# A fixed order for the DMA queue, value sums in skewed quads, first weights on another queue, and scan banks apart, in a one-core scan-and-attention kernel

## The chip, the core and the metric

The kernel runs on one core of a Trainium2 chip. The metric is the device time of one execution in microseconds (us), as the median of several executions. The profile shows one execution; its span is about 1.5 to 1.7 us shorter than the time reported for the same execution.

The engines in the profile are: PE, the tensor engine's matmuls, and PEld, its weight loads; DVE, VectorE; ACT, ScalarE; POOL, GpSimd. SP is the Sync engine, which computes nothing here but issues nearly all DMAs. SPq and ACTq are the DMA issues on the Sync and the ScalarE queue. A DMA queue issues in order, as the traces here show it: an issue that has to wait for its data holds up all issues behind it (in e1 below, eight stores wait behind two copies until 119.3 us).

Executions of the kernel before differ by up to 3% among themselves (163.8 to 168.5 us over all chips used). Those over 1.5% above the fastest of their group are called slow and are left out of ratios; the slow ones show a mean granted tensor clock of 0.954 to 0.974 in the records, the fast ones mostly 0.976 to 0.988.

## The reference

Two independent parts read two inputs of 2048 positions by 448 features and write the two halves of one output.

```python
# part A: a diagonal complex state space, 448 states
Lam_bar = exp(dt * Lam)
Bu = x @ B_bar.T                       # complex
h_t = Lam_bar * h_{t-1} + Bu_t         # 2048 steps
a = 2 * real(h @ C.T) + x * Dskip
# part B: 16 heads of 28; each position sees 8 positions, 2 apart, backwards
q, k, v = split(x @ wqkv)
logits[s, w] = q[s] . k[s - 2*w] * scale      # w = 0..7, masked before the start
o[s] = sum_w softmax(logits)[s, w] * v[s - 2*w]
b = o @ wo
out = concatenate([a, b], axis=-1)
```

## The kernel before

The instructions of the tensor engine, VectorE and ScalarE are issued in the order in which the program calls them. The Sync queue is not in that list: a scheduler of the build chooses its order.

```python
with tc.manual_schedule(engines={ET.PE, ET.DVE, ET.Activation}):
    plan(a, b, cx, pool)
```

The loads at the start: three small parameter vectors and the skip vector on the ScalarE queue, all else on the Sync queue. `load_w(1)` and `load_w(0)` bring the key and query weights, each as a main DMA of 336 KB and a tail of 56 KB.

```python
    a.load_params()        # prow x3, drow x2, on nc.scalar
    b.load_x(0)            # two transposing DMAs
    b.load_w(1)
    b.load_w(0)
    b.load_x(1)
    # ... x 2 and 3, B, value weights, 32 transposing loads of A's x
```

The value projection writes `vd`, 16 positions to a partition, plus a halo of 14 that is copied from the neighbour partition by DMA (`halo`). The second copy is called after the last value projection, and after it come 8 loads of C and 24 small loads of wo.

```python
            b.proj_v(j, "A")
            if j == 8:
                b.halo(b.vd, 8, HALO)
            if j == 0:
                b.halo(b.vd, 0, 8)
                a.load_c()
                b.load_wo()
                a.setup_c()
```

The value sums on VectorE: for a block of positions, 8 products of attention weight and value, each added to the sum right after it is made. The first block has 8 positions (3584 elements a partition, called 8-wide below), then follow blocks of 4, 2 and 2. When a block is done, `turn` sends it through a transposing DMA into `oT` for the output projection.

```python
        acc = self.pvb[:, j0:j1]
        for w in range(W):
            off = HALO + j0 - DIL * w
            t_ = self.pvt[w % 2][:, 0:n] if w else acc
            V.tensor_tensor(t_, self.at[:, w, j0:j1, :].unsqueeze(2).to_broadcast([NCH, n, DH, H]),
                            self.vd[:, off:off + n], op=ALU.mult)
            yield
            if w:
                V.tensor_tensor(acc, acc, t_, op=ALU.add)
                ...   # turn at w == W - 1
                yield
    pv = chain(b.pv(0, 8), b.pv(8, 12), b.pv(12, 14), b.pv(14, 16))
```

The second half of the plan puts steps of `pv` between those of part A: local products (`u_ps`), the scan (`last`, `rot`, `scan`, `back`), corrections (`co`), outputs of A (`y`) and of B (`out`). The outputs of A leave through two buffers `ya`, those of B through two buffers `yb`.

```python
    run(pv, 6)
    loc((2, 4), (2, 5))
    r = a.regs("g3")              # PSUM banks of the scan, from the pool "mm" of the local products
    a.last(r[0])                  # -> rt on VectorE
    loc((1, 4), (1, 5), (0, 6), (2, 6))
    r_ = a.regs("rot")
    a.rot(r_[0], 0)
    # ... scan, back, groups, correct, with run(pv, 1) or run(pv, 2) between
    run(pv, 5)
    for a_ in range(4):
        a.y(a_, 3)
    a.correct(2, "A", range(7))
    for a_ in range(4):
        a.y(a_, 1)
    run(pv, 30)
    b.out(0)
    b.out(2)
    # ... y(.,0), out(4), out(6), out(8), out(10), y(.,2), out(12)
    run(pv, 99)
    b.out(14, "AV")
```

## Time and profile before

| | before |
|---|---|
| time, median of the first 3 runs | 165.15 us (165.13 to 167.45) |
| span of the profiled execution | 163.7 us |
| PE busy / DVE busy | 144.1 / 133.1 us |
| longest DVE wait after 10 us | 8.3 us, for the halo copy |
| longest PE wait after 10 us | 6.3 us, for scan inputs of DVE |
| DVE ends its value sums | 155.9 us |

First the busy times by stretch of the kernel before. Each row is a stretch in us from the span's start, its length, then the busy us of PE, PEld, DVE, ACT and POOL with the number of instructions, the granted clock, the DMA share and GB/s.

```profile
20.00:50.00 30.00, 29.84 (x219) 16.13 (x217) 27.06 (x34) 20.96 (x41) 0.00 (x0) 1.00 0.35 66
...
73.00:84.00 11.00, 11.00 (x53) 4.95 (x52) 2.74 (x3) 6.13 (x11) 0.00 (x0) 1.00 0.44 108
84.00:94.00 10.00, 4.47 (x33) 2.33 (x31) 9.93 (x7) 2.66 (x5) 0.00 (x0) 0.83 0.78 171
94.00:105.00 11.00, 9.26 (x56) 5.04 (x57) 9.96 (x13) 3.53 (x6) 0.00 (x0) 0.84 0.01 1
...
118.00:146.00 28.00, 27.62 (x179) 14.94 (x177) 27.52 (x32) 14.76 (x29) 0.00 (x0) 1.00 0.52 124
```

A different engine is full in each part. From 20 to 50 us it is PE (29.84 of 30). From 73 to 84 PE is full and DVE does 2.74 us of work in 11. From 84 to 94 it is the other way round, and in 94 to 105 the clock has fallen to a mean of 0.84. From then on DVE is nearly full. An average over the span (PE 88%, DVE 81%) hides that for 20 us one of the two always stood.

The waits tell why. The lines name who waited, for whom, the total in us, how often, and the longest.

```profile
DVE pvt L273 <- DMA vd<-vd: 8.3, 1, 8.3
...
PE u_ps L524 <- DVE rt L557: 6.3, 1, 6.3
...
PE gt L588 <- DVE gsc L572: 1.5, 1, 1.5
...
DVE gsc L572 <- PE rotA L565: 1.0, 1, 1.0
```

And the chain that ended last shows the cause (start, length, what), cut to a few pieces between 64 and 86 us:

```profile
65.50 0.61 SPq L342
...
67.53 0.64 SPq L123
...
78.25 0.60 SPq L186
...
78.90 4.46 DMA vd<-vd
...
83.46 2.04 DVE pvt L273
```

L342 are loads of C, L123 to L125 those of wo, L186 is the halo copy. The queue was issuing loads whose data PE first uses at 118.3 us (C) and 134.0 us (wo), while the copy that DVE needed at 75 us stood behind them. DVE then makes its products from 83.5 us on, and the scan inputs, which come after six of its steps, are late. On PE that looks like this (start, length, engine, line, operation, tiles, shapes; in brackets the idle time before and what ended it):

```profile
87.45 1.03 PE L524 MATMUL u_ps<-xaT,Bcat 128*128 128x512 bf16 x4
94.73 1.89 PE L524 MATMUL u_ps<-xaT,Bcat 128*128 128x512 bf16 x4 [6.26 <-DVE rt L557]
```

Four such matmuls take 1.03 us before the 6.3 us hole and 1.89 us after it. These are local products, which read nothing of the scan (their inputs are xaT and Bcat). By the kernel, their sums and the scan's share the four PSUM banks of "mm"; so what they waited for was most likely a bank that stayed full until DVE had read the scan's sum.

The start, in the chain of waits:

```profile
0.80 4.47 DMA xbT<-in_B_x_dram
...
5.28 3.99 DMA wqkv_nat<-in_B_wqkv_dram
...
9.32 5.40 PE qk_ps L168 x24
```

The DMAs of x and then of the weights hold the start; the projections are in full swing only at 9.3 us, when the last weights have landed.

### The profile page before, as it was taken

What the parts mean: (1) busy time and instruction counts of PE and PEld (TensorE: products, weight loads), DVE (VectorE), ACT (ScalarE), POOL (GpSimd) and SP (SyncE); (2) the same over time, 40 slices, a digit from 0 to 9 for tenths busy, and PEclk for the clock granted to TensorE, in tenths of its full rate; (3) what the DMA queues carried; (4) which work ended last, traced back from release to release, by engine and by line L of the source; (5) the groups of instructions that cost most, each with busy time, mean ns of one, the idle gap of its engine ahead of it and who ended that gap; (6) DMA issues with size and microseconds to landing.
All of it is one profiled execution on the core that took longest, in us unless ns stands there. A gap on an engine that the chain in (4) does not pass through costs nothing.

```text
span 163.7 us, 2533 instructions
## 1 busy us (share of the span) xinstructions
PE 144.1 (88%) x934; PEld 78.3 (48%) x934; DVE 133.1 (81%) x167; ACT 87.2 (53%) x162; POOL 10.8 (7%) x46
## 2 busy tenths in 40 slices
PE   6799799999999999999996089639899999999980
PEld 4346454555555665554452044515454555555540
DVE  0479998599999997493069979999999999999911
ACT  3158965686768577545554014208834745545360
POOL 8960000000000002000000000000000000000000
PEclk9999999999999999999999559999999999999998
DMA  5899982221222226632669400000009622946231
GB/s 100 215 201 193 228 136 58 45 63 35 62 57 40 45 55 107 112 77 52 175 165 207 95 0 0 4 0 0 0 30 162 149 84 84 224 144 175 80 114 56
DMA packets 42284, 15.67 MB, mean 96 GB/s; under 512 B 34771, under 2 KB 42017, under 8 KB 42271
## 3 DMA queue, kind: packets, MB, share of 16 engines
q1 hardware_dynamic: 42200, 15.50, 43.0%
q8 instruction: 7, 0.11, 0.3%
q14 instruction: 6, 0.05, 0.1%
q10 hardware_dynamic: 71, 0.01, 0.0%
HBM read 3.62 MB, written 3.67 MB: 45 GB/s over the span
## 4 chain that ended last, share of the span: by engine, by line
PE 51%; DVE 20%; DMA 10%; SPq 7%; issue 5%; ACT 4%; DVEq 0%; ACTq 0%
PE qk_ps L168 15%; PE y_ps L624 11%; PE wo_ps L305 8%; DVE pvt L273 6%; DVE pvb L277 4%; PE lg L214 4%; DVE pr L203 3%; PE co L599 3%; PE v_ps L182 3%; DMA xbT<-in_B_x_dram 3%; DMA vd<-vd 3%; DVE mat L482 2%; DMA wqkv_nat<-in_B_wqkv_dram 2%; SPq L125 2%; DMA out_dram<-ya 2%
## 5 line engine op out<-in xcount | busy, mean ns | idle before, releaser
L203 DVE TENSOR_TENSOR pr<-qT,kT 112x4096 bf16<-112x4096 bf16 (+1 forms) x20 | 36.2, 1859 | 3.5 <-PE lg L214 2.6
L273 DVE TENSOR_TENSOR pvt<-attn,vd 128x896 bf16<-128x896 bf16 (+2 forms) x28 | 30.4, 1084 | 8.3 <-DMA vd<-vd 8.3
L524 PE MATMUL u_ps<-xaT,Bcat 128*128 128x512 bf16 x112 | 28.4, 389 | 6.3 <-DVE rt L557 6.3
L168 PE MATMUL qk_ps<-xbT,wqkv_nat 128*112 128x512 bf16 x128 | 29.7, 382 | 2.3 <-DMA wqkv_nat<-in_B_wqkv_dram 1.3
L277 DVE TENSOR_TENSOR pvb<-pvb,pvt 128x896 bf16<-128x896 bf16 (+2 forms) x28 | 30.5, 1090 | 0.9
L624 PE MATMUL y_ps<-C,u 128*128 128x448 bf16 x112 | 23.8, 353 | 0.0
L168 PEld LDWEIGHTS <-wqkv_nat 128*112 128x112 bf16 x128 | 15.9, 130 | 15.1 <-issue 3.4
L532 ACT CAST u<-u_ps 128x512 bf16<-128x512 f32 x21 | 12.3, 586 | 16.5 <-PE u_ps L524 11.8
L524 PEld LDWEIGHTS <-Bcat 128*128 128x128 bf16 x112 | 10.7, 100 | 18.5 <-DVE rt L557 6.7
L627 ACT CAST ya<-y_ps 128x448 bf16<-128x448 f32 x16 | 8.5, 532 | 16.0 <-PE y_ps L624 14.0
L607 ACT CAST u<-co 128x512 bf16<-128x512 f32 x21 | 10.8, 618 | 7.1 <-PE co L603 7.1
L182 PE MATMUL v_ps<-wqkv_nat,xbT 128*128 128x448 bf16 x64 | 13.8, 358 | 0.0
L305 PE MATMUL wo_ps<-wo_p,oT 128*128 128x448 bf16 x64 | 13.1, 352 | 0.7 <-ACT oT L296 0.7
L624 PEld LDWEIGHTS <-u 128*128 128x128 bf16 x112 | 9.9, 98 | 7.3
L81 ACT CAST qT<-qk_ps 112x512 bf16<-112x512 f32 x16 | 9.3, 588 | 5.8 <-PE qk_ps L168 5.8
L81 ACT CAST vd<-v_ps 128x448 bf16<-128x448 f32 x16 | 8.5, 538 | 5.1 <-PE v_ps L182 5.1
L182 PEld LDWEIGHTS <-xbT 128*128 128x128 bf16 x64 | 8.8, 147 | 5.0 <-issue 2.5
L81 ACT CAST kT<-qk_ps 112x512 bf16<-112x512 f32 x16 | 9.2, 587 | 3.3 <-PE qk_ps L168 3.3
L81 ACT CAST yb<-wo_ps 128x448 bf16<-128x448 f32 x15 | 8.0, 532 | 4.1 <-PE wo_ps L305 3.6
L599 PE MATMUL co<-u,ident 128*128 128x512 bf16 x21 | 7.9, 378 | 2.1 <-DVE u L590 1.0
L214 PE MATMUL lg<-pr,onesW 112*32 112x512 bf16 x128 | 9.5, 383 | 0.2 <-DVE pr L203 0.2
L305 PEld LDWEIGHTS <-oT 128*128 128x128 bf16 x64 | 6.2, 97 | 6.7 <-ACT oT L296 0.9
(155 smaller groups left out, 153.3 us busy)
## 6 DMA issues: line engine op xcount, KB each, us to landing
out_dram<-ya SPq DMA_DIRECT2D x16, 112.0 KB, 1.7
out_dram<-yb SPq DMA_DIRECT2D x8, 224.0 KB, 2.3
wqkv_nat<-in_B_wqkv_dram SPq DMA_DIRECT2D x3, 336.0 KB, 3.7
vd<-vd SPq DMA_DIRECT2D x1, 784.0 KB
wo_p<-in_B_wo_dram SPq DMA_DIRECT2D x16, 42.0 KB, 1.9
vd<-vd SPq DMA_DIRECT2D x1, 588.0 KB, 4.9
xaT<-in_A_x_dram SPq DMA_TRANSPOSE x32, 2.4
bX<-in_A_B_re_dram SPq DMA_DIRECT2D x1, 392.0 KB, 5.6
```

The source lines that it names most:

```text
L81: nc.scalar.copy(out, in_)
L168: nc.tensor.matmul(ps[:], lhsT=self.wn[:, k, which, g * KP:(g + 1) * KP], rhs=self.xT[:, k, c * CH:(c + 1) * CH], start=(k == 0), stop=(k ...
L182: nc.tensor.matmul(ps[:], lhsT=xv[:, k, j, :], rhs=self.wn[:, k, 2, :], start=(k == 0), stop=(k == KT - 1))
L203: self.nc.vector.tensor_tensor(pr[:, :, g0:g1, :], self.qT[:, c, g0:g1].unsqueeze(1).to_broadcast([KP, 2, n, CH]), ks, op=ALU.mult)
L214: nc.tensor.matmul(lg[NW * g:NW * (g + 1), :], lhsT=self.onesW[:, NW - 4 - 4 * w:2 * NW - 4 - 4 * w], rhs=pr[:, i, g, :], start=(w == 0), ...
L273: V.tensor_tensor(t_, self.at[:, w, j0:j1, :].unsqueeze(2).to_broadcast([NCH, n, DH, H]), self.vd[:, off:off + n], op=ALU.mult)
L277: V.tensor_tensor(acc, acc, t_, op=ALU.add)
L305: nc.tensor.matmul(ps[:], lhsT=oT[:, NSL * (i // 2) + 3 * n + k, :], rhs=self.wo_p[:, KT * n + k, :], start=(k == 0), stop=(k == KT - 1))
L524: nc.tensor.matmul(ps4[:], lhsT=self.Bcat[:, k, m, :], rhs=self.xT[:, b, k], start=(k == 0), stop=(b % 2 == 0 and k == KT - 1))
L532: nc.scalar.copy(self.h[b][:, m, :], ps)
L599: nc.tensor.matmul(ps, lhsT=cx.ident[:], rhs=h_, start=True, stop=False)
L624: nc.tensor.matmul(ps[:], lhsT=self.state(m, a, b), rhs=self.C[:, m, :], start=False, stop=(m == NM - 1), skip_group_check=True)
```

## The change

Its intent, part by part: (1) the Sync queue issues in program order too; (2) the first weights go out on the ScalarE queue, in front of the parameters, and the three tails become one DMA; the first projections run without the tail first; (3) the value sums are made in blocks of 4 from the start (quads), with the product of the next step issued before the add of this one (skew), so that an add does not follow its own product; more, smaller steps let two output pairs of B move into the gaps of the scan; (4) the scan's PSUM banks come from another pool than those of the local products. The `ya` buffers become three. The diff, cut:

```diff
-        self.nc.sync.dma_start(self.wn[:, 0:3, which, :], v[0:3 * NCH]...)
-        self.nc.sync.dma_start(self.wn[PL:NCH, 3, which, :], v[3 * NCH:D])
+        q.dma_start(self.wn[:, 0:3, which, :], v[0:3 * NCH]...)
+    def load_wt(self):
+        self.nc.sync.dma_start(self.wn[PL:NCH, 3], v[3 * NCH:D])
 ...
-        for w in range(W):
-            ...                             # product w, then add w
+        def buf(w):
+            return self.pvt[w % 2][:, w // 2 % 2 * 4:][:, 0:n]
+        mult(0)
+        yield
+        mult(1)
+        yield
+        for w in range(1, W):
+            if w < W - 1:
+                mult(w + 1)
+                yield
+            V.tensor_tensor(acc, acc, buf(w), op=ALU.add)
 ...
-        psA = self.cx.ps([NCH, MA, NCH], f32, nm + "A", "mm")
+        psA = self.cx.ps([NCH, MA, NCH], f32, nm + "A", "pt")
 ...
-        ya = pool.tile([NCH, D], bf16, name="ya", tag="ya", bufs=2)
+        ya = pool.tile([NCH, D], bf16, name="ya", tag="ya", bufs=3)
 ...
+    b.load_w(1, nc.scalar)
     a.load_params()
+    b.load_w(0, nc.scalar)
+    a.load_skip()
     b.load_x(0)
-    b.load_w(1)
-    b.load_w(0)
+    b.load_wt()
 ...
-    with tc.manual_schedule(engines={ET.PE, ET.DVE, ET.Activation}):
+    with tc.manual_schedule(engines={ET.PE, ET.DVE, ET.Activation, ET.SP}):
 ...
     cx.warm(12, "cols")
-    cx.warm(8, "rows")
+    cx.warm(3, cols=CH)
     a.params()
+    cx.warm(4, cols=CH)
 ...
-    run(proj(0), 8)
+    first = [(g, which) for which in (1, 0) for g in (0, 1)]
+    for g, which in first:
+        b.proj_m(0, g, which, range(3))     # without the tail
+    for g, which in first:
+        b.proj_m(0, g, which, [3])
+        b.proj_e(0, g, which, "A")
 ...
-    pv = chain(b.pv(0, 8), b.pv(8, 12), b.pv(12, 14), b.pv(14, 16))
+    pv = chain(b.pv(0, 4), b.pv(4, 8), b.pv(8, 12), b.pv(12, 14), b.pv(14, 16))
 ...
-    run(pv, 6)
+    run(pv, 12)
 ...
+    a.groups(range(0, 2))
+    b.out(0)
     a.rot(r_[1], 0)
     a.scan(r_[1])
-    a.groups(range(0, 4))
+    a.groups(range(2, 4))
+    b.out(2)
 ...
-    run(pv, 5)
     for a_ in range(4):
         a.y(a_, 3)
+    run(pv, 7)
     a.correct(2, "A", range(7))
     for a_ in range(4):
         a.y(a_, 1)
-    run(pv, 30)
-    b.out(0)
-    b.out(2)
-    ...
+    run(pv, 15)
     b.out(4)
     b.out(6)
-    ...
+    for a_ in range(4):
         a.y(a_, 0)
+    run(pv, 15)
     b.out(8)
```

More of the change, by code (lines that the diff above doesn't have):

```diff
@@ L95, in __init__ @@
         self.B_x, self.B_wqkv, self.B_wo, self.out_b = B_x, B_wqkv, B_wo, out_b
-        self.lg, self.oT = {}, {}
+        self.lg, self.oT, self.ps_t = {}, {}, {}
     def load_x(self, c):
@@ L104, in load_x, with load_w @@
         self.nc.sync.dma_start_transpose(out=self.xT[:, 3, sl], in_=x_[:, D - NCH:D])
-    def load_w(self, which):
+    def load_w(self, which, q):
         if which == 1:
@@ L110, in load_w @@
         v = self.B_wqkv.rearrange("r (w c) -> r w c", w=3)[:, which, :]
-        self.nc.sync.dma_start(self.wn[:, 0:3, which, :], v[0:3 * NCH].rearrange("(k p) c -> p k c", p=NCH))
-        self.nc.sync.dma_start(self.wn[PL:NCH, 3, which, :], v[3 * NCH:D])
+        q.dma_start(self.wn[:, 0:3, which, :], v[0:3 * NCH].rearrange("(k p) c -> p k c", p=NCH))
+    def load_wt(self):
+        v = self.B_wqkv.rearrange("r (w c) -> r w c", w=3)
+        self.nc.sync.dma_start(self.wn[PL:NCH, 3], v[3 * NCH:D])
     def load_wo(self):
@@ L164, in proj_t, with proj_m, proj_e @@
     def proj_t(self, c, g, which, eng):
-        nc = self.nc
-        ps = self.cx.ps([KP, CH], f32, "qk_ps", "mm")
-        for k in range(KT):
-            nc.tensor.matmul(ps[:], lhsT=self.wn[:, k, which, g * KP:(g + 1) * KP],
-                             rhs=self.xT[:, k, c * CH:(c + 1) * CH], start=(k == 0), stop=(k == KT - 1))
+        self.proj_m(c, g, which, range(KT))
+        self.proj_e(c, g, which, eng)
+    def proj_m(self, c, g, which, ks):
+        if ks[0] == 0:
+            self.ps_t[g, which] = self.cx.ps([KP, CH], f32, "qk_ps", "mm")
+        for k in ks:
+            self.nc.tensor.matmul(self.ps_t[g, which][:], lhsT=self.wn[:, k, which, g * KP:(g + 1) * KP],
+                                  rhs=self.xT[:, k, c * CH:(c + 1) * CH], start=(k == 0), stop=(k == KT - 1))
+    def proj_e(self, c, g, which, eng):
+        ps = self.ps_t[g, which]
         if which == 0:
@@ L269, in pv, with mult @@
         acc = self.pvb[:, j0:j1]
-        for w in range(W):
+        def buf(w):
+            return self.pvt[w % 2][:, w // 2 % 2 * 4:][:, 0:n]
+        def mult(w):
             off = HALO + j0 - DIL * w
-            t_ = self.pvt[w % 2][:, 0:n] if w else acc
-            V.tensor_tensor(t_, self.at[:, w, j0:j1, :].unsqueeze(2).to_broadcast([NCH, n, DH, H]),
+            V.tensor_tensor(buf(w) if w else acc,
+                            self.at[:, w, j0:j1, :].unsqueeze(2).to_broadcast([NCH, n, DH, H]),
                             self.vd[:, off:off + n], op=ALU.mult)
-            yield
-            if w:
-                V.tensor_tensor(acc, acc, t_, op=ALU.add)
-                if w == W - 1:
-                    for j in range(j0, j1, 4):
-                        (self.turn if j1 < T else self.turn_p)(j, min(j1, j + 4))
-                yield
+        mult(0)
[7 more added lines that the diff above has]
+            V.tensor_tensor(acc, acc, buf(w), op=ALU.add)
+            if w == W - 1:
+                for j in range(j0, j1, 4):
+                    (self.turn if j1 < T else self.turn_p)(j, min(j1, j + 4))
+            yield
     def turn(self, j0, j1):
@@ L325, in load_params, with load_skip @@
             nc.scalar.dma_start(self.prow[i * NM:(i + 1) * NM], v)
-        Dk = self.A_Dskip
+    def load_skip(self):
+        nc, Dk = self.nc, self.A_Dskip
         nc.scalar.dma_start(self.drow[0:3, :], Dk[0:3 * NCH].rearrange("(k p) -> k p", p=NCH))
@@ L377, in params @@
         lre, lim = ll[:, 0], ll[:, 1]
-        ptd = self.cx.ps([NCH, KT], bf16, "pt_d", "lg")
-        nc.tensor.transpose(ptd[:], self.drow[:], ident[0:KT, 0:KT])
-        dsk = sm("dsk", (NCH, KT))
-        V.tensor_copy(dsk[:], ptd[:])
         kv = pool.tile([NCH, NPW, NM], f32, name="kv")
@@ L396, in params, with skip @@
         V.tensor_scalar(rden[:], rden[:], 2.0, None, op0=ALU.mult)
-        self.Dm, self.dsk, self.at2, self.kv = Dm, dsk, at2, kv
+        self.Dm, self.at2, self.kv = Dm, at2, kv
         self.lre, self.lim, self.rden = lre, lim, rden
         self.mats = {}
+    def skip(self):
+        ptd = self.cx.ps([NCH, KT], bf16, "pt_d", "pt")
+        self.nc.tensor.transpose(ptd[:], self.drow[:], self.cx.ident[0:KT, 0:KT])
+        self.dsk = self.pool.tile([NCH, KT], f32, name="dsk")
+        self.nc.vector.tensor_copy(self.dsk[:], ptd[:])
     def tables(self):
@@ L534, in regs @@
     def regs(self, nm):
-        psA = self.cx.ps([NCH, MA, NCH], f32, nm + "A", "mm")
-        psB = self.cx.ps([NCH, NM - MA, NCH], f32, nm + "B", "mm")
+        psA = self.cx.ps([NCH, MA, NCH], f32, nm + "A", "pt")
+        psB = self.cx.ps([NCH, NM - MA, NCH], f32, nm + "B", "pt")
         return (psA, 0, MA), (psB, MA, NM)
@@ L648, in body @@
     a.load_b()
-    b.load_w(2)
+    b.load_w(2, nc.sync)
     for b_ in range(4):
@@ L668, in plan, with proj @@
     cx.warm(12, "cols")
-    cx.warm(8, "rows")
+    cx.warm(3, cols=CH)
     a.params()
-    def proj(c):
-        for g in (0, 2):
+    cx.warm(4, cols=CH)
+    def proj(c, gs=(0, 2)):
+        for g in gs:
             for which in (1, 0):
@@ L695, in plan @@
     run(tb)
-    run(proj(0), 8)
+    first = [(g, which) for which in (1, 0) for g in (0, 1)]
[4 more added lines that the diff above has]
+        b.proj_e(0, g, which, "A")
+    p0 = proj(0, (2,))
+    run(p0, 4)
     run(tb)
@@ L703, in plan @@
                 run(tb)
+                a.skip()
     run(fill, 8)
@@ L761, in plan @@
     a.rot(r_[0], 0)
-    run(pv, 1)
+    run(pv, 3)
     a.scan(r_[0])
-    loc((3, 4), (3, 5), (1, 6), (3, 6))
-    run(pv, 2)
-    a.last(r[1])
+    loc((3, 4), (3, 5), (1, 6))
     rb = a.regs("bak")
     a.back(rb[0])
-    run(pv, 1)
+    loc((3, 6))
+    run(pv, 5)
+    a.last(r[1])
+    run(pv, 2)
+    a.groups(range(0, 2))
+    b.out(0)
     a.rot(r_[1], 0)
     a.scan(r_[1])
-    a.groups(range(0, 4))
-    run(pv, 2)
-    a.correct(1, "A", range(0, 2))
+    a.groups(range(2, 4))
+    b.out(2)
+    run(pv, 1)
+    a.correct(1, "A", range(0, 4))
     a.back(rb[1])
-    a.correct(1, "A", range(2, 4))
     a.correct(0, "A", range(0, 2))
@@ L787, in plan @@
         a.y(a_, 1)
-    run(pv, 30)
-    b.out(0)
-    b.out(2)
-    for a_ in range(2):
-        a.y(a_, 0)
+    run(pv, 15)
     b.out(4)
     b.out(6)
-    for a_ in range(2, 4):
+    for a_ in range(4):
         a.y(a_, 0)
+    run(pv, 15)
     b.out(8)
```

## The prediction

> **What bounds the kernel now.** Span 163.7 us (reported 165.15). By a table of busy time per stretch the tensor engine is full early (29.8 of 30 us from 20 to 50, 14.7 of 15 from 50 to 65), and VectorE from 83.5 to the end (9.93 of 10, 9.96 of 11, 6.97 of 7, 11.7 of 12, 9.6 of 10). Between lies the largest hole: the list of waits shows VectorE idle 8.3 us before the second value product, until the halo copy vd<-vd landed. The last value projection was evicted at 63 us, but the chain of waits shows the Sync queue issuing the loads of C and wo (24 small ones, 0.43 us each) from 65.5 to 78.2, and only then that copy, 4.5 us to landing. The tensor engine pays later: idle 6.3 us (88.5 to 94.7) for VectorE's scan inputs, then a granted clock of about a half (four matmuls 1.89 us, not 1.03), then 4.4 us in small waits. At the start it waits for DMA: first projections at 7.0, in full swing at 9.3.
>
> **What the change does.**
> 1. Sync issues in program order: halo copies before the loads of C and wo. Landing at about 67, needed at 72: the 8.3 us go. The loads land near 85; C is used past 105.
> 2. First weights on ScalarE's queue. The page shows the DMA engines 90 to 100% busy from 2 to 9 us, and the Trainium skill (DMA: Bandwidth & Descriptors, Issuing engines are not separate DMA queues) says a second issuer saves only issue time. All must still land by 8.5 to 9, but 12 matmuls without the tail start near 6: about 15 instead of 8 done by 9.3, 1.5 us at 0.217. VectorE's table chain, ending near 11, takes some back: 1.2.
> 3. Quads, skewed. An add that needs the product before it starts 0.11 us later than an independent one (pairs of 8 columns 4.00 us, 4 2.13, 2 1.19). Skewing saves 0.11 x 21 = 2.3, less 0.3 for 15 more instructions: 2.0. Quads also let two output pairs (3.06 us of matmuls) fill the tensor engine's scan holes.
> 4. Scan banks leave four banks to the local products; the rotA wait (1.0) shrinks.
>
> **Critical path.** VectorE ended its sums at 155.9. Minus 8.3, 1.2, 2.0, 1.0, plus 1.5 for a wait I see where group sums 4 to 6 are issued too late for it: 144.9. Then 6.5 us of tail (7.8 before, 1.1 of it waiting for the tensor engine): 151.4. The tensor engine alone (160.0, less 12.5 idle, 2 low clock, 1.2 start, plus 3 of new waits and 3.7 tail) gives 151. Two engines with equal ends push each other: span 152, plus 1.5 between span and time: **153.5 us, range 150.5 to 157.5**. Faster by over 2%: 0.95; within: 0.04; slower: 0.01.
>
> **Right if:** no VectorE wait on vd; no tensor-engine gap over 3 us after 10 us, hence no low clock mid-kernel (the Trainium skill, TensorE: Matmul & The Clock Gate, part 1, has one idle window of about 3.4 us halve the clock; before's trace agrees: 6.3 us idle, then half); pairs near 2.02 and 1.08; first projection near 6 us; y starting near 110, not 118.
>
> **Wrong if:** the weights' tail lands after 9.5; stores sit behind oT transposes in the fixed order, so that output buffers stall the tensor engine; skewed pairs cost as before; group corrections wait over 2 us on VectorE.

## The result, and the profile after

| | before | after |
|---|---|---|
| time, median of all runs to that point | 166.3 us (165.13 to 168.47) | 156.59 us (156.44 to 158.02) |
| span of the profiled execution | 163.7 us | 154.8 us |
| ratio of fast runs | | 0.947 (95%: 0.937 to 0.957) |
| mean granted clock of the profiled execution | 0.975 | 1.0 |
| DVE ends its value sums | 155.9 us | 146.9 us |
| first use of C (y) | 118.1 us | 110.7 us |

A ratio is the mean time of one kernel's fast runs over that of the other's in the same rounds, so it is not quite the ratio of the medians given beside it. The time fell by 5.3%, inside the stated range.

The busy times by stretch of the changed kernel, same columns as before:

```profile
73.00:84.00 11.00, 11.00 (x52) 4.98 (x51) 10.97 (x14) 5.86 (x10) 0.00 (x0) 1.00 0.41 83
84.00:94.00 10.00, 10.00 (x72) 5.47 (x70) 9.73 (x15) 4.89 (x9) 0.00 (x0) 1.00 0.64 128
94.00:105.00 11.00, 9.17 (x65) 5.08 (x63) 10.97 (x18) 4.89 (x10) 0.00 (x0) 1.00 0.21 59
...
118.00:146.00 28.00, 25.79 (x171) 14.07 (x169) 27.93 (x42) 12.91 (x26) 0.00 (x0) 1.00 0.45 120
```

From 73 to 94 us both engines are now full at the same time: DVE does 10.97 us in 73 to 84 where it did 2.74, PE 10.00 in 84 to 94 where it did 4.47, and the clock stays at 1.00. The last row is the new loss: PE did 25.79 of 28 us, having done 27.62 before.

The waits of the changed kernel:

```profile
ACT L396 <- DMA drow<-in_A_Dskip_dram: 6.6, 1, 6.6
...
ACT ya L651 <- DMA out_dram<-ya: 3.8, 1, 3.8
...
PE wo_ps L325 <- ACT yb L81: 1.7, 1, 1.7
...
DVE u L614 <- PE gt L612: 1.2, 1, 1.2
```

The wait for vd and the wait for rt are not there any more. New are ScalarE waits: 6.6 us at its first table load, behind the issue of the skip vector, and 3.8 us for the stores of `ya`; behind the latter PE waited 1.7 us. The Sync queue in order of time shows the halo copy (L196, L197) before the loads of C (L364):

```profile
62.26 0.60 SPq L196 DMA_DIRECT2D vd<-vd  x1
...
63.84 1.33 SPq L196 DMA_DIRECT2D vd<-vd  x1
...
66.09 4.43 SPq L364 DMA_DIRECT2D cn<-in_A_C_re_dram  x4
...
130.70 1.53 SPq L307 DMA_TRANSPOSE oT<-pvb  x1
132.33 1.55 SPq L328 DMA_DIRECT2D out_dram<-yb  x2
133.97 4.98 SPq L652 DMA_DIRECT2D out_dram<-ya  x4
```

The last three of these lines are the new wait: stores of B and A (L328, L652) stand behind a transposing copy (L307) that could not be issued before DVE's third quad was done at 130.6 us.

The start, in the chain of waits:

```profile
0.80 5.21 DMA xbT<-in_B_x_dram
...
6.03 0.26 ACTq L349
...
6.33 0.44 DMA drow<-in_A_Dskip_dram
6.77 0.17 PE pt_p L394
6.93 0.97 PE warm L66 x4
7.90 3.45 PE qk_ps L175 x16
```

The first projections run from 7.7 us without a break, where they ran at 7.0 and then from 9.3 before. But the transposed parameters (pt_p) come at 6.8 us, at 5.9 before. (pt_p reads the parameters and not the skip vector, although the profile names the skip vector's load, drow, as what it waited for; in e7, with the same start, it names the third parameter load, landed at 6.53 us.) VectorE makes the tables from the parameters ahead of its first query-key product. This table chain starts at 8.13 us, at 6.33 before, because ScalarE prepares its input and had to load its function table first: that load ran from 6.62 to 7.90 us, behind the skip vector's issue (L349), which the chain above has waiting for the first transposed x, landed at 6.00; why it waited for that was not tested. The product starts at 12.83 us, at 11.91 before. The fourth chunk's logits are transposed at 62.66 us, at 62.35 before: the start has gained nothing.

### The profile page after: what moved, and what is told of

The parts are those of the page before. It is cut to its first block, busy times and chain, and to the rows that moved or that the text cites. A ratio compares the mean times of both kernels' runs of the same rounds, so it can differ in the third digit from the quotient of the medians.

```text
span 154.8 us, 2545 instructions
## 1 busy us (share of the span) xinstructions
PE 142.7 (92%) x933; PEld 77.6 (50%) x933; DVE 132.4 (86%) x182; ACT 86.7 (56%) x162; POOL 8.9 (6%) x46
## 4 chain that ended last, share of the span: by engine, by line
PE 72%; DVE 11%; DMA 6%; ACT 4%; issue 4%; ACTq 0%; DVEq 0%
PE qk_ps L175 16%; PE u_ps L548 15%; PE y_ps L648 13%; PE wo_ps L325 6%; PE lg L224 4%; DMA xbT<-in_B_x_dram 3%; DVE pr L213 3%; PE v_ps L192 3%; DVE mat L506 3%; DMA out_dram<-ya 3%; PE co L623 3%; PE u_ps L551 2%; PE y_ps L645 2%; PE co L627 2%; PE gt L612 1%
## 5 line engine op out<-in xcount | busy, mean ns | idle before, releaser
L297 DVE TENSOR_TENSOR pvb<-pvb,pvt 128x1792 bf16<-128x1792 bf16 (+1 forms) x35 | 31.4, 898 | 0.2
L285 DVE TENSOR_TENSOR pvt<-attn,vd 128x1792 bf16<-128x1792 bf16 (+1 forms) x35 | 31.0, 897 | 0.0
L548 PE MATMUL u_ps<-xaT,Bcat 128*128 128x512 bf16 x112 | 27.3, 379 | 0.0
```

Of the source, the lines that this page charges most:

```text
L285: V.tensor_tensor(buf(w) if w else acc, self.at[:, w, j0:j1, :].unsqueeze(2).to_broadcast([NCH, n, DH, H]), self.vd[:, off:off + n], op=AL ...
L297: V.tensor_tensor(acc, acc, buf(w), op=ALU.add)
L548: nc.tensor.matmul(ps4[:], lhsT=self.Bcat[:, k, m, :], rhs=self.xT[:, b, k], start=(k == 0), stop=(b % 2 == 0 and k == KT - 1))
```

## The experiments

All kernels gave the right result. Three groups of four ran each on one chip, with the kernel before beside them: a0, e5, e7 and e10; e1, e2, e3 and e8; e6, e9, e11 and e12. The first run of the first group is the changed kernel again, as a yardstick. The other two groups have no such run, so there a difference to a0 is one between chips and may be off by about 0.7 us: the fastest run of the kernel before was 163.82, 164.55 and 163.81 us on the three.

### a0_changed_again

No edit.

> The changed kernel itself once more, as the yardstick of this chip for the three runs beside it: 156.4 to 156.8 us, first projection matmul at 7.7 us, first query-key product on VectorE at 12.8, tensor engine waiting 1.7 us before the second half of output pair 8-10 at 137.3 to 139.1.

Measured: 156.32 us (156.18 to 156.49, 6 runs), ratio 0.951. The wait near 138 is there (1.5 us for oT and 0.7 us for yb in this execution). Its runs spread over 0.31 us, so differences of 0.5 us between kernels of this group can be read.

### e1_order_only: the fixed order alone, on the kernel before

```diff
-    with tc.manual_schedule(engines={ET.PE, ET.DVE, ET.Activation}):
+    with tc.manual_schedule(engines={ET.PE, ET.DVE, ET.Activation, ET.SP}):
-    run(pv, 30)
+    run(pv, 15)
     b.out(0)
 ...
+    run(pv, 15)
     b.out(8)
```

The second edit calls the first outputs of B behind fewer of the sums, as the change does.

> The kernel before with only the Sync queue's order fixed (and the last three groups of value sums called where the change calls them, since the old calls would deadlock in a fixed order). Theory: the fixed order alone takes the 8.3 us wait on the halo copy away and carries most of the change: 157.5 to 159.5 us, no low clock. Rival: without quads the scan inputs still come late and the tensor engine holes absorb it: 162 us or more.

Measured: 164.58 us (163.58 to 165.31), ratio 0.994 (0.982 to 1.006). The theory's number is missed by over 5 us. But the rival's reason is missed as well: the 8.3 us wait is gone, the scan inputs come at 85.4 us, and DVE makes its first corrections 8 us earlier. What was gained was lost later. The longest PE wait and the queue behind it, in the list of waits and then on the Sync queue:

```profile
PE co L599 <- ACT ya L627: 4.4, 1, 4.4
```

```profile
114.42 4.74 SPq L287 DMA_TRANSPOSE oT<-pvb  x2
119.26 13.30 SPq L628 DMA_DIRECT2D out_dram<-ya  x8
```

In program order the two transposing copies of the 8-wide sums (L287) stand ahead of the eight stores of `ya` (L628). DVE finishes these sums at 114.4 us. The first `ya` was ready at 112.5, both buffers were full at 114.1, ScalarE waited 7.2 us for a buffer and PE 4.4 us for ScalarE, and then came the low clock (0.50 from 122 to 124 us). So an order can be right at one place and wrong at the next. The new theory: the fixed order carries most of the gain, if the stores do not stand behind sums that are still being made. It is tested next.

### e11_order_stores: as e1, with the first stores ahead of the copies

```diff
 (e1_order_only, and)
-    run(pv, 5)
     for a_ in range(4):
         a.y(a_, 3)
+    run(pv, 5)
```

This changes no order on DVE or PE; it changes the place of four stores on the Sync queue.

> The kernel before with the Sync order fixed as in e1_order_only (164.58 us) and, besides, the first four y rounds called ahead of the last 8-wide value sums, so that their stores stand on the Sync queue ahead of the two transposing copies that wait for those sums until 114.4 us. Theory: e1 lost its 8 us because ScalarE waited 7.2 us for the y stores behind those copies, and the tensor engine 4.4 us plus a spell of low clock behind ScalarE. Then the wait goes and the time is 157 to 159 us. Rival: the 8-wide sums themselves (scan inputs and transposed copies late) are what costs, and the wait only moves to another place: 162 us or more.

Measured: 159.48 us (159.29 to 160.63), ratio 0.971 (0.963 to 0.979). The 4.4 us wait is 0.7 us now:

```profile
PE co L599 <- ACT ya L627: 0.7, 1, 0.7
```

The time is half a microsecond above the range of the theory and well below the rival's. So the fixed order, with stores kept clear, is worth about 5.7 us of the 8.8 us of the whole change (165.15 and 156.32, against 159.48; by the ratios 2.9 of 4.9%, where only two runs of the kernel before beside it were fast). DVE ends its sums at 148.6 us here, PE starts the last transposes at 152.2: PE is the later one, likely since two output pairs (3.06 us) still stand at the end and its waits of 1.5, 1.0 and 0.8 us around the scan remain. (The trace is of the slowest of the six, 160.63 us, which ran with a mean clock of 0.93 from 90 to 115 us.) What the rest of the change adds, 3.2 us, is quads, skew, the earlier output pairs, the third `ya` buffer and the new order of calls around the scan together; the last two were never undone alone.

### e2_no_order: all of the change but the fixed order

```diff
-    with tc.manual_schedule(engines={ET.PE, ET.DVE, ET.Activation, ET.SP}):
+    with tc.manual_schedule(engines={ET.PE, ET.DVE, ET.Activation}):
```

> The changed kernel with the Sync queue left to the scheduler again. Theory: the second halo copy falls behind the small output-weight loads again, VectorE waits 7 to 8 us for vd near 75 to 83, and the time is 162.5 to 164.5 us. Rival: quads and skew carry the change: below 160.

Measured: 165.21 us (165.0 to 165.52), ratio 0.997. The wait is back, longer than before, and with it the late scan inputs. With the banks apart, PE now waits at the matmuls that read these inputs (rotA) and no longer at the local products:

```profile
DVE pvt L285 <- DMA vd<-vd: 9.5, 1, 9.5
...
PE rotA L587 <- DVE rt L580: 6.2, 1, 6.2
```

All other parts together are worth nothing without this one (0.7 us beyond the theory's range, on its side). Neither the order alone nor the rest alone moves the time by 2%; together they take 5.3%.

### e3_no_skew: products directly ahead of their adds

```diff
         for w in range(1, W):
-            if w < W - 1:
-                mult(w + 1)
-                yield
             V.tensor_tensor(acc, acc, buf(w), op=ALU.add)
             ...
             yield
+            if w < W - 1:
+                mult(w + 1)
+                yield
```

> The changed kernel with each product issued directly ahead of the add that needs it (same quads, same number of steps). Theory: each of 35 adds, or the 33 newly dependent, starts 0.11 us later, VectorE ends its sums about 3.0 us later than 146.9; 1.2 us of that hides behind the tensor engine, so 158.2 to 158.8 us. Rival: the skew saves nothing on VectorE and the time stays at 156.5.

Measured: 158.82 us (158.31 to 160.3), 2.5 us over a0 by the medians, 2.1 by the fastest runs; the theory's range holds, at its upper edge. DVE ends its sums at 150.1 us instead of 146.9, 3.1 us later where 3.0 was expected. The groups of instructions of DVE in the changed kernel, then in this one, show that no instruction is longer by more than 7 ns; the idle time ahead of the adds (the last number) is what differs:

```profile
L297 DVE TENSOR_TENSOR pvb<-pvb,pvt 128x1792 bf16<-128x1792 bf16 x21 | 22.8, 1085 | 0.1
...
L297 DVE TENSOR_TENSOR pvb<-pvb,pvt 128x896 bf16<-128x896 bf16 x14 | 8.6, 618 | 0.1
```

```profile
L294 DVE TENSOR_TENSOR pvb<-pvb,pvt 128x1792 bf16<-128x1792 bf16 x21 | 22.9, 1091 | 0.7
...
L294 DVE TENSOR_TENSOR pvb<-pvb,pvt 128x896 bf16<-128x896 bf16 x14 | 8.8, 625 | 0.5
```

The rest of the difference is overlap: an instruction that depends on nothing just made starts about 0.08 us before the one ahead of it has ended. The starts of skewed adds and products are 1.00 us apart with 1.08 us each. How the loss reaches the time is in the profiled execution: a copy into `oT` comes later, PE waits 2.4 us for it (until 138.2 us), and then the clock is at 0.50 from 140 to 142 us. The one run without a lowered clock took 158.31 us.

### e8_out_late: output pairs 0 and 2 out of the scan's gaps

```diff
     a.groups(range(0, 2))
-    b.out(0)
 ...
     a.groups(range(2, 4))
-    b.out(2)
 ...
+    b.out(0)
+    b.out(2)
     run(pv, 15)
     b.out(4)
```

> The changed kernel with output pairs 0 and 2 (3.06 us of matmuls) called after the second round of y instead of in the scan's gaps. Theory: the gaps open again (waits of 1 to 3 us on scan inputs between 97 and 105) and the tensor engine, which bounds the tail, ends 2 to 3 us later: 158 to 159.5 us. Rival: the matmuls only move, the tail has slack: 156.5 to 157.

Measured: 160.56 us (159.54 to 160.8), 4.2 us over a0 by the medians and 3.4 by the fastest runs, 1.1 us above the theory's range. The gaps of PE open (1.4, 1.2 and 0.6 us), and without the two pairs the clock falls too:

```profile
100.00:104.00 4.00, 2.38 (x15) 1.28 (x15) 4.00 (x8) 0.00 (x1) 0.00 (x0) 0.77 0.00 0
104.00:107.00 3.00, 2.38 (x6) 0.65 (x5) 2.97 (x6) 1.66 (x3) 0.00 (x0) 0.50 0.00 0
```

Part of the rest is not the edit's: in the profiled execution the four warming matmuls at 6.9 us take 1.89 us instead of 1.04, and the logits of the fourth chunk are transposed 1.5 us later than in the changed kernel. See e9 for such starts. The profiled execution is 3.9 us longer than a0's; less 1.5 for the start, 2.4 us are the edit's, or up to 3.4 if the fastest run had no such start, which left no trace.

### e9_banks_back: scan sums in the banks of the local products

```diff
-        psA = self.cx.ps([NCH, MA, NCH], f32, nm + "A", "pt")
-        psB = self.cx.ps([NCH, NM - MA, NCH], f32, nm + "B", "pt")
+        psA = self.cx.ps([NCH, MA, NCH], f32, nm + "A", "mm")
+        psB = self.cx.ps([NCH, NM - MA, NCH], f32, nm + "B", "mm")
```

> The changed kernel with the scan's sums back in the four banks that local products use. Theory: the local products then wait for VectorE to read the scan sums, as the 6.3 us hole in before did, by 0.5 to 1.5 us, and the time is 157 to 158. Rival: with quads the scan inputs are read at once and the banks do not matter: 156.1 to 156.7.

Measured: six executions in two clusters, 156.43, 156.58, 156.67 and 158.26, 158.32, 158.35. The median (157.47) lies in the theory's range, but it means nothing here. The profile fell on one of the upper cluster, and there the loss is all at the start:

```profile
7.00:9.00 2.00, 2.00 (x7) 0.89 (x7) 0.93 (x8) 0.92 (x2) 1.66 (x7) 0.61 1.26 190
9.00:11.00 2.00, 2.00 (x6) 1.03 (x5) 1.90 (x6) 0.33 (x2) 0.00 (x0) 0.54 0.53 112
```

The clock was at about a half from 7 to 11 us, the fourth chunk's logits are transposed at 64.41 us instead of 62.66, and nothing more is lost from there on. The lower cluster is where the changed kernel is. So the rival holds for it: no cost of the banks is seen. No wait of a local product for a bank appears in the trace either. One wait is new: the group sums (gt, also in the pool "mm") stood 1.7 us, until 103.1 us, for DVE's reading of earlier ones, which is what a lack of banks would do. The 1.5 us that PE waited for DVE and ScalarE at this stage in the changed kernel are gone instead, so the end is not moved. That the other two executions of the upper cluster started the same way, and that the 158.02 us of the changed kernel was one, is likely but not shown, since they left no trace.

### e6_start_undone: first weights back on the Sync queue

```diff
-    b.load_w(1, nc.scalar)
     a.load_params()
-    b.load_w(0, nc.scalar)
     a.load_skip()
     b.load_x(0)
+    b.load_w(1, nc.sync)
+    b.load_w(0, nc.sync)
     b.load_wt()
```

> The changed kernel with all first weights back on the Sync queue and the parameters alone on ScalarE's. Theory: moving the issue bought nothing (third matmul stretch ends within 0.5 us in before and after, DMA engines full either way): 156.0 to 156.9 us, transposed maxima of the fourth chunk at 62.2 to 63.0. Rival: the move gained what was predicted and something else lost it: 157.3 us or more.

Measured: 156.09 us (155.54 to 156.16), ratio 0.948 (0.943 to 0.954). The transposed logits come at 62.43 us. Moving the issue is worth nothing; the 0.2 us the other way are between two chips. The theory holds.

### e5_params_first: parameters ahead of the weights

```diff
-    b.load_w(1, nc.scalar)
     a.load_params()
+    b.load_w(1, nc.scalar)
     b.load_w(0, nc.scalar)
-    a.load_skip()
     b.load_x(0)
     b.load_wt()
     b.load_x(1)
+    a.load_skip()            # now on nc.sync
```

> The changed kernel with the three small parameter loads ahead of the first weights on ScalarE's queue and the skip-vector loads later on the Sync queue. Theory: the start gained nothing because the parameters queued behind 336 KB of weights and ScalarE's sequencer stood at the skip-vector issue until 6.6 us, so the table load, the table chain and VectorE's first product (12.8 us, 11.9 before) came late. Then: table load near 3.5, parameter transpose before 6.2, first product near 11.3, the value sums about 1 us earlier and 155.3 us. Rival: the DMA engines are full and the tensor engine bounds the stretch to 65 us anyhow: first product earlier, but time still 156.3 to 156.7.

Measured: 156.8 us (156.53 to 157.7), 0.5 us over a0. Half of the theory came true: the table load starts at 3.05 us, the parameters are transposed at 5.87. But VectorE's first product starts at 13.19, later than the changed kernel's 12.83, because now the projections wait:

```profile
2.08 0.40 ACTq L111
...
2.51 6.80 DMA wqkv_nat<-in_B_wqkv_dram
...
9.36 2.37 PE qk_ps L175 x10
```

The query weights, issued at 2.5 us, landed at 9.3. With the skip vector gone from the ScalarE queue, the next x transposes went out earlier (4.16 us instead of 4.72, and 6.68 instead of 8.92), into DMA engines that were already full. Which of the two moves delayed the weights is not settled. Both theory and rival missed their numbers; the step that was wrong in the theory is that only the parameters stood in the way.

### e7_stores_first: stores ahead of the third quad's copy

```diff
-    run(pv, 15)
     b.out(4)
     b.out(6)
+    run(pv, 15)
     for a_ in range(4):
         a.y(a_, 0)
```

> The changed kernel with the third quad's value sums called after output pairs 4 and 6, so that on the Sync queue their stores stand ahead of the transposing copy that waits for VectorE until 130.6 us. Theory: the 1.7 us wait of the tensor engine near 138 comes from stores standing behind that copy: the wait shrinks below 0.5, VectorE's end at 146.9 becomes the limit and the time falls by 1.0 to 1.3 to about 155.3. Rival: the stores are slow for their own bandwidth (3.99 us in the chain): wait stays over 1.2, time within 0.3 of 156.5.

Measured: 155.36 us (155.18 to 155.62), 0.96 us under a0. The wait of PE for ScalarE has shrunk (0.5 us for oT stand beside it):

```profile
PE wo_ps L325 <- ACT yb L81: 0.4, 1, 0.4
```

The last output pair but one, out(12), ends at 147.0 us with DVE's sums at 146.9: the two ends meet. The theory holds. The store of `ya` still takes 4.34 us in the chain where the median is 1.7, right behind a transposing copy; why it is slow there was not tested.

### e10_start_stores: e5 and e7 together

> Both edits together. If both theories hold they add up, since one moves VectorE's sums and the other the tensor engine's tail: 153.8 to 154.5 us. If only the tail edit works, as the other: 155.3. If VectorE's sums do not come earlier, 155.3 too, with VectorE ending at 146.9.

Measured: 156.03 us (155.82 to 156.31). The gain of e7 less the loss of e5: 155.36 + 0.5 is 155.9. All the numbers expected (155.3 us at most) were missed, since none reckoned with a loss in e5. Within the noise the edits add up, and e5's does harm.

### e12_stores_no_warm: e7 without the second warming

```diff
 (e7_stores_first, and)
     a.params()
-    cx.warm(4, cols=CH)
```

> The run e7_stores_first (155.36 us) without the four warming matmuls that stand between the parameter transpose and the first projection. Theory: in the chain of waits the first projection at 7.7 to 7.9 waits for the parameters (landed at about 6.6, behind the weights on the same queue) and 0.97 us of warming, not for weights: it starts near 6.9, VectorE's slack of 1.9 us later passes it on, and the time is 154.4 to 154.9. Rival: weights or x land no earlier, or the clock drops: 155.2 to 155.6.

Measured: 154.75 us (154.62 to 154.88), ratio 0.940 (0.935 to 0.946): the fastest version, 1.6 us under the changed kernel (e9's faster runs on the same chip, 156.4 to 156.7, say that the chip is not the reason). The first projection starts at 7.01 us. In the chain of waits the start is now held by weights:

```profile
2.85 5.72 DMA wqkv_nat<-in_B_wqkv_dram
...
8.62 2.37 PE qk_ps L175 x10
```

So of 0.97 us of warming taken away, the DMA gives back all but 0.3 at the fourth chunk (62.27 against 62.55 us in e7); the median fell by 0.6 us, on another chip, and the profiled executions differ by 0.3.

## Why the prediction was right, point by point

The time is in the range, 0.9 us from its upper end, and the two ends it was built from are of the right kind, but the span is 2.8 us longer than the 152 of the sum: 11.65 us were promised from 165.15 and 8.6 came. The large errors all lie on one side, and it is the width of the range that takes them in. Where these went, by the terms of the sum:

1. **"Sync issues in program order ... the 8.3 us go."** Right. The copies are issued at 62 to 66 us, VectorE does not wait for vd, and e2 brings the wait back (9.5 us) with the whole time. What the prediction did not say: the order alone is worth little (e1, 164.58), since it puts stores behind sums; the change is fast because it also calls the stores early. With that single correction the order is worth about 5.7 us (e11). The prediction had that mechanism among its ways to be wrong, but gave it no term.

2. **"All must still land by 8.5 to 9 ... 1.2."** Wrong, and the largest error in the sum: predicted minus 1.2, measured plus 0.3 at the fourth chunk (62.66 against 62.35), and e6 shows no gain in the time. The step that failed is "12 matmuls without the tail start near 6". PE has its instructions in order, and before the projections stand the parameter transpose and four warming matmuls. The parameters were issued behind 336 KB of weights on the same queue and were used at 6.8 us; with the warming, projections began at 7.7. Without that warming they began at 7.0 and then waited for weights until 8.6 (e12). The table chain, which the prediction left near 11, ended at 12.7 us: the skip vector's issue, now behind the second weights on ScalarE's queue, went out at 6.03 us where it had gone at 2.1, and ScalarE's table load stood behind it. VectorE's first product became 0.9 us later. With the first weights back on the Sync queue (e6) the chain is early again, and that product still comes at 12.60, waiting for the projections. The Trainium skill (DMA: Bandwidth & Descriptors, Issuing engines are not separate DMA queues) agrees: a second issuing queue brought nothing that can be read (e6 is 0.2 us the faster one). Its section Queues, rings and completion order says that each DMA engine consumes a queue's descriptors in ring order; that agrees with the late parameters: in e7 the third of them, 1.8 KB, issued at 2.29 us behind the weights, took 4.24 us to land.

3. **"Quads, skewed ... 2.0."** Right in kind, the size a little large. Pairs are 2.00 us (2.02 predicted) and 1.07 us (1.08). From 155.9 to 146.9 VectorE gained 8.9 us; taking the halo (8.3), the rotA wait (1.0), the start (plus 0.3), the group wait (plus 1.2) and a 0.2 us wait for g3A away leaves 1.4 us for quads and skew, where 2.0 was predicted. By blocks: the last eight columns took 31.6 us where they took 33.8, 2.2 less; the first eight, waits left out, took 0.9 us more as quads than 8-wide, and the prediction had only 0.3 for the added instructions. Undoing the skew alone costs VectorE 3.1 us (e3), so the quads themselves would have cost about 1.7 without it. **"Quads also let two output pairs fill the scan holes"** is right: undone, it costs 2.4 to 3.4 us (e8).

4. **"Scan banks ... the rotA wait (1.0) shrinks."** The wait is gone, but not by the banks: with the banks back the lower cluster of e9 is as fast, and its trace has no such wait. What removed it was not isolated; the change also calls three steps of VectorE (3.2 us) between the scan's inputs and the scan, where before it was one (2.0 us).

5. **"Plus 1.5 for a wait I see"** where group sums 4 to 6 come too late: measured 1.2.

6. **Tail 6.5 us.** Measured 7.8, from 146.9 to the end at 154.8, as PE was 1.2 us behind VectorE. The cause is the 1.7 us wait behind the stores, named under "wrong if" and not counted in the sum; e7 takes 1.0 us of the time back by moving one call.

Together: the start is 1.5 us off, the tail 1.3, the quads 0.6. That is the whole 3.4 us by which the span exceeds the sum of 151.4; the step from 151.4 to 152, for two equal ends, covered 0.6 of it. The clock part was right: no low clock in the middle of the profiled execution (1.0, 0.975 before). The Trainium skill (TensorE: Matmul & The Clock Gate, Part 1: The HAM clock gate) has one idle window of about 3.4 us halve the clock, and the holes of 6.3 us before and 4.4 us in e1 agree. It also came after shorter ones (e3, e8, e9; see the end), so the "hence" of the prediction, no gap over 3 us and so no low clock, is not a rule that these runs bear out.

## What to carry to other kernels

Before costing an edit to a busy engine, read the queue that feeds it: here 8 us of VectorE time hung on the order of a few DMA issues, and an in-order queue must be checked twice, for a needed copy behind loads that can wait, and for a ready store behind a copy whose data is still being made. Parts of a change can be worth nothing alone and all of it together, so undo each from the whole and add each to the old. When DMA engines are full at the start (a mean share of 0.91 from 2 to 9 us in the kernel before), changing who issues or in what order moves the wait from one load to another; fewer bytes before the first matmul may gain there, but no run here tried it.

## What the Trainium skill lacked or had wrong

- VectorE: DVE Perf Modes, The DRAIN you can't avoid, says that in a chain of copies a semaphore after each costs nothing extra, and its rules for authors say to minimise the number of operations, not the waits. The section also says that an operation which is not held starts earlier, but gives no size. Here an add directly behind its own product starts 1.12 us after that product starts (4-wide, in the kernel before), and 1.00 us when another instruction stands between; undoing the skew cost VectorE 3.1 us and the kernel 2.1 to 2.5 us (e3), with the same number of instructions.
- TensorE: Matmul & The Clock Gate, Part 1, ties the half clock to an idle window of about 3.4 us. It came here with shorter gaps: in e9 after one of 1.74 us near the start (clock 0.61, then 0.54), while a gap of 1.61 us at the same place in a0 left it at 1.00; in e3 after one of 2.4 us (0.50 from 140 to 142 us); in e8 after gaps of 1.2 and 1.4 us close together (0.50 from 104 to 107 us). The page does say that the window runs freely and, further on, that short idles between groups of matmuls can make the clock swing; it gives no figure for how short.
- The same Part 1 warns that the clock's events in a trace can be unreliable, without a case of a slow stretch that is missing. Here is one: in e8 the clock column is 1.00 from 7 to 9 us, while the four warming matmuls there took 1.89 us in place of 1.04.
- The same Part 1 says that the number of slow matmuls at the start varies from run to run, at a cost under 1% of a typical kernel's span. The one traced execution of e9's upper cluster lost 1.75 us by a low clock in its first 11 us, 1.1% of its span. No page says that a kernel's executions can then fall in clusters (156.4 to 156.7 and 158.3 to 158.4 us in e9), so that a median of six lies where no execution is.
- No page has the loss from a store that is ready but stands behind a transposing copy on the same issuing queue: 7.2 us of ScalarE and 4.4 us of PE in e1.
